# A store of 13 rows is sent as seven blocks of partitions

## The chip, the cores and the metric

The kernel runs on one core of a Trainium2 chip. The metric is device time in microseconds of one execution. A core has compute engines (TensorE or PE, VectorE or DVE, ScalarE or ACT, GpSimd or POOL), a queue engine SyncE or SP that issues transfers here, and 16 DMA engines that move data between HBM and SBUF. SBUF has 128 partitions.

## The reference

A channel attention: the mean over all pixels of each channel is scaled by one weight, put through a sigmoid, and multiplied into the input.

```python
g = jnp.einsum("bhwc->bc", x) / (H * W)
gp = jnp.pad(g, ((0, 0), (pad, pad)))
s = jnp.zeros_like(g)
for i in range(k):
    s = s + gp[:, i:i + C] * w1d[i]
s = _sigmoid(s)
return x * s[:, None, None, :]
```

`x` is bfloat16 of 1 x 384 x 384 x 384, 113.25 MB; `k` is 1. The output has the same shape. No output can be written before all of `x` has been read once, and `x` does not fit into SBUF as it is.

## The kernel before, in words

The 147,456 pixels are dealt to the 128 partitions, 1152 to each; the kernel calls one pixel of every partition a row, so a row is 128 x 384 bfloat16 values, 98,304 bytes, 768 bytes in a partition. One large SBUF tile, `arena`, has 275 rows. The rows are split into two chunks: `STREAMED` rows (785) are read twice, `KEPT` rows (367) are read once and stay on the chip, most of them with four rows folded into three (`fold`, and `unfold` in pass two), 71 of them raw.

Pass one loads everything and sums it on TensorE (`sum_rows`, L253), while DVE and ACT fold the kept rows. Then one sigmoid gives the scale `s_bf` (L443). Pass two (from L451) multiplies rows in place with `scale` (DVE, three pieces on POOL) and writes them out with `store`; rows that become free are filled by `load` with streamed rows, which are scaled and stored in turn.

The order of pass two comes from the planner loop at L688. It steps a model clock `now` in units of `DT`, with its own costs (`ROW`, `PER_STORE`, `TT`, `TS`), and decides what DVE does next and when SP issues which load or store. Every transfer of pass two is issued by SP, in the order in which the planner made it, through one queue. `landed` holds the rows ready to be scaled: first `Y`, `U`, `T` and `V` (4 or 8 rows each), then the first two slots of 13 rows, at `A` and `A + 13`. `send` puts a store in `waiting`, and L714 takes it from there when the model's DVE is done.

`Flow.add` (L34) works out what each step waits for from the arena rows that it reads and writes: a load waits for every earlier store that reads the rows that it overwrites. Each transfer has one of 24 semaphore lanes, and waits for the transfer 24 before it (L50). Waits of a transfer stand in SP's queue ahead of it (L111), so what is behind waits too. A transfer's semaphore rises by 16 and is complete when all of its DMA engines have landed their share.

The store of the change is the first of 13 rows in pass two: chunk `KEPT`, arena rows `A` to `A + 13`, `lo == raw(A)`. In the profile it is the ninth store of pass two, issued by SP at 278.31 us. Behind it SP issues a load of 8 rows (278.69 us), the 5 rows that POOL scaled (279.54 us), the next 13-row store (280.98 us), a load of 8 rows (281.90 us), and the load of 13 rows that overwrites the slot of the changed store (284.53 us), which waits for that store's landing.

Of the kernel before, what the change touches and what calls it, by code (L numbers as in the profile page):

```python
# [127 lines left out]
def kernel(  # L128
# [11 lines left out]
    nc = tc.nc  # L140
    P = nc.NUM_PARTITIONS
# [18 lines left out]
    A = V + PAIR  # L160
# [27 lines left out]
    arena = pool.tile([P, ROWS, C], bf16, name="arena")  # L188
# [11 lines left out]
    of = out.rearrange("b h w c -> (b h w) c")  # L200

    def view(t, r0, n):
        return t[r0 * P : (r0 + n) * P, :].rearrange("(p r) c -> p r c", r=n)

    def rows(lo, n):
        return [("a", r) for r in range(lo, lo + n)]

    fl = Flow(nc, tc)
# [6 lines left out]
    STREAMED, KEPT = (0, N_STREAM), (N_STREAM, N_KEPT)  # L215
# [8 lines left out]
    def raw(a):  # L224

        return c_raw + (a - U if a < G0 else PAIR + a - V)
# [65 lines left out]
    def fold(k):  # L292
# [46 lines left out]
        reads=["ones", "w_bf"], writes=["bank0"],  # L339
# [4 lines left out]
        reads=["bank0"], writes=["w_sc"],  # L344
# [39 lines left out]
    def copy_bank(i, src, dst, reads, writes):  # L384
        fl.add(
            "ACT", lambda: nc.scalar.copy(dst.bitcast(u32), src.bitcast(u32)), reads=reads, writes=writes  # L386
        )

    for i, bk in enumerate(banks):
        lo, hi = i * BANK, min((i + 1) * BANK, PS * C)  # L390
# [46 lines left out]
    for a, n in S2 + [(U, 8)] + S3 + S1 + [(V, 8), (Y, 8), (T, 5), (T + 5, 3)]:  # L437
# [6 lines left out]
        reads=["bank0", "w_sc"], writes=["s_bf"],  # L444
# [6 lines left out]
    def scale(a, n, eng="DVE", s=s_bf, after=()):  # L451
        v = arena[:, a : a + n, :]
        vec = nc.vector if eng == "DVE" else nc.gpsimd
        fl.add(
            eng,
            lambda: vec.tensor_tensor(  # L456
                out=v, in0=v, in1=s[:, None, :].to_broadcast([P, n, C]), op=Op.mult
            ),
            reads=rows(a, n) + ["s_bf" if s is s_bf else "bank0"], writes=rows(a, n), after=after,
        )  # L460

    def store(chunk, a, lo, hi):
        r0, n = chunk
        return fl.add(
            "SP",
            lambda: nc.sync.dma_start(out=view(of, r0, n)[:, lo:hi, :], in_=arena[:, a : a + hi - lo, :]),
            reads=rows(a, hi - lo), dma=True,
        )

    def unfold(k, first):  # L470

# [36 lines left out]
    def TT(n):  # L508
        return 0.15 + 0.2 * n
# [70 lines left out]
    def runs():  # L580
        got, i = [], 0
        while i < ROWS:
            if idle[i]:
                j = i
                while j < ROWS and idle[j]:
                    j += 1
                got.append((j - i, i))
                i = j
            else:
                i += 1  # L590
        return got

    def send(chunk, a, lo, hi, then, known=None):

        waiting.append((dve_at, hi - lo, then, chunk, a, lo, [] if known is None else known))

    def backlog():
        return sum(e[1] for e in moves) + ROW * sum(e[1] for e in waiting)
# [10 lines left out]
    def stored(a, n):  # L609

        def f():
            for i in range(a, a + n):
                for left in needed:
                    left.discard(("a", i))
                if not Y <= i < Y + 8 and not U <= i < U + 8 and not V <= i < V + 8:
                    idle[i] = True
        return f
# [30 lines left out]
    def start_group():  # L648

        if not line:  # L650
            return False
        g = line[0]
        column = home[g]
        if needed[column] or not free[column] or g == BANKED and (bank_at is None or now < bank_at[1]):
            return False
        line.popleft()
        free[column] = False
        a, q = GROUPS[g]
        if g == BANKED:
            a = bank_at[0]  # L660

        below = 0
        if column < 2 and g != COLUMNS[column][0]:
            below = GROUPS[COLUMNS[column][COLUMNS[column].index(g) - 1]][1]

        def part():
            release(a + below, sent - below)

        def done():
            nonlocal out_rows  # L670
            out_rows += 1
            free[column] = True
            release(a + max(below, sent), 4 * q - max(below, sent))

        for k in of_group(g):
            fields, three, fourth = unfold(k, a)
            turns.extend((fields + (None,), three + (None,), fourth + (None,)))
        sent = 0
        if len(line) >= total - N_SPLIT and q == PAIR:

            f, t, _ = turns[-5]
            sent = 3 * PIECE
            turns[-5] = (f, t, lambda: send(KEPT, a, c_group[g], c_group[g] + sent, part, written))
        f, t, _ = turns[-1]
        turns[-1] = (f, t, lambda: send(KEPT, a + sent, c_group[g] + sent, c_group[g] + 4 * q, done, written))
        return True

    while True:  # L688

        if dve_at <= now:  # L690
            ahead = backlog()
            can = bool(turns)
            if not can and not alongside and (ahead >= PENDING or not landed):
                can = start_group()
            if landed and (ahead < PENDING or not can):
                chunk, a, lo, n, end = landed.popleft()
                scale(a, n, s=s_ps if alongside and now else s_bf)
                dve_at = now + TT(n)
                since = (a, lo) if since is None else since
                if end or ahead < MERGE:  # L700
                    b, first = since
                    send(chunk, b, first, lo + n, stored(b, lo + n - first))
                    since = None
            elif can:
                f, t, then = turns.popleft()
                f()
                dve_at = now + t
                if then:
                    then()
        if alongside and alongside[0][0] <= now:  # L710
            _, chunk, a, lo, n = alongside.popleft()
            store(chunk, a, lo, lo + n)
            moves.append([now + LAT, n * ROW + PER_STORE, stored(a, n)])
        while waiting and waiting[0][0] <= now:  # L714
            _, n, then, chunk, a, lo, known = waiting.popleft()
            known.append(store(chunk, a, lo, lo + n))
            moves.append([now + LAT, n * ROW + PER_STORE, then])
        if not asked and not line and not turns:
            verdict()
            asked = True  # L720
        if out_rows == total and not checked:
            checked = True
            fl.add("POOL", again, reads=["odd_i", "s_bf"], writes=rows(Y, N_OVER), after=written)
        while over and over[0][0] <= now:
            over.popleft()[1]()

        got = runs()
        if bank_at is None and len(line) <= total - BANKS_AT and got and max(got)[0] >= PS * 4 // 3:
            a = max(got)[1]
            for i in range(a, a + PS * 4 // 3):  # L730
                idle[i] = False
            back = arena[:, a : a + PS, :].rearrange("p r c -> p (r c)")
            for i, bk in enumerate(banks):
                lo, hi = i * BANK, min((i + 1) * BANK, PS * C)
                copy_bank(i, bk[:, 0 : hi - lo], back[:, lo:hi], [("bank", i)], rows(a, PS))
            bank_at = (a, now + 5.0)
            got = runs()

        if got and todo < N_STREAM:
            n, a = max(got)  # L740
            n = min(n, CAP, N_STREAM - todo)
            ahead = backlog()
            if n >= BIG or n == N_STREAM - todo or (ahead < LOW and n >= 8) or ahead < LAST:
                load(STREAMED, a, todo, todo + n)
                for i in range(a, a + n):
                    idle[i] = False
                parts = [(STREAMED, a + e, todo + e, f - e, f == n) for e, f in split(n, PART)]
                todo += n
                moves.append([now + LAT, n * ROW + PER_LOAD, lambda parts=parts: landed.extend(parts)])

        if moves and moves[0][0] <= now:
            moves[0][1] -= DT
            if moves[0][1] <= 0:
                over.append((now + SEEN, moves.popleft()[2]))
        else:
            stall += DT
        if not (alongside or moves or waiting or over or landed or line or turns) and todo == N_STREAM:
            break
        now += DT
# [34 lines left out]
```

## Time and profile before

| What | Value |
|---|---|
| Time, median of 3 runs | 720.96 us (720.65, 720.96, 723.42) |
| Span of the profiled execution, first to last instruction | 719.4 us |
| Its own time outside the span | not recorded; the median is 1.6 us over the span |
| HBM read, written | 190.41 MB, 113.25 MB |
| Mean rate over the span | 422 GB/s |
| Busy: DVE, PE, ACT | 69%, 30%, 16% |
| Last landing of pass one; sigmoid | 267.1 us; 268.1 us |
| First store of pass two issued | 269.73 us |
| Changed store: issued, landed | 278.31 us, 284.5 us |
| Last store: issued, landed | 681.40 us, 717.6 us |

How to read it: times are from the start of the span. A stretch of the span has the busy time of each engine, the share of time for which the 16 DMA engines were busy on the mean, and the rate at which they moved bytes. A transfer has its issue in SP's queue, and a landing, which is that of its last DMA engine. The trace also holds a record for each landing of each transfer (one per DMA engine, without the engine's number) and for each packet (here one partition's part of a transfer).

### The profile page before, as it was taken

The page shows a single profiled execution, that of the slowest core. Times are in us where ns is not written, and L with a number is a line of the kernel's source. Part 1 is how long each engine was busy: PE and PEld are TensorE (multiplying, and loading weights), DVE is VectorE, ACT ScalarE, POOL GpSimd, SP SyncE. Part 2 cuts the span into 40 slices and gives each one's busy share as a digit, 9 for nine tenths or more (in the row PEclk, how much of TensorE's full clock was granted, in tenths as well). Part 3 has the DMA queues.
Part 4 walks back from the last instruction along what each step waited for, and adds up shares of the span by engine and source line. Part 5 has one row for each costly group of instructions (what it writes and reads, how often), then busy time and mean ns, then how long its engine had stood idle before and what let it go on. Part 6 is the DMA issues. An engine that isn't in the chain of part 4 may idle for free.

```text
span 719.4 us, 2061 instructions
## 1 busy us (share of the span) xinstructions
PE 213.0 (30%) x1202; PEld 0.3 (0%) x3; DVE 493.9 (69%) x471; ACT 115.7 (16%) x93; POOL 10.6 (1%) x7
## 2 busy tenths in 40 slices
PE   4677788897987770000000000000000000000000
PEld 0000000000000000000000000000000000000000
DVE  4600004788999719988999998999998985095500
ACT  3600003566677610002000000000000000000000
POOL 0000000000000005000000000000000000000000
PEclk9899999999999995555555555555555555555555
DMA  9999999999999979999999999999999999999997
GB/s 379 435 433 435 426 428 435 438 434 425 426 426 429 427 326 376 421 391 423 430 430 437 430 428 441 428 433 435 430 436 433 429 437 428 441 432 427 440 439 314
DMA packets 20174, 303.79 MB, mean 422 GB/s; under 512 B 2243, under 2 KB 2243, under 8 KB 6083
## 3 DMA queue, kind: packets, MB, share of 16 engines
q1 hardware_dynamic: 20160, 303.67, 99.0%
q8 instruction: 4, 0.07, 0.0%
q14 instruction: 8, 0.06, 0.0%
q10 hardware_dynamic: 2, 0.00, 0.0%
HBM read 190.41 MB, written 113.25 MB: 422 GB/s over the span
## 4 chain that ended last, share of the span: by engine, by line
DMA 63%; DVE 23%; PE 6%; ACT 2%; another core or an unknown queue 1%; SPq 1%; issue 0%; DVEq 0%
DMA arena<-in_x_dram 42%; DMA out_dram<-arena 20%; DVE arena L456 16%; PE bank L242 6%; DVE arena L276 4%; DVE arena L282 3%; ACT arena L313 2%; SPq L236 1%; ACT s_bf L443 0%; SPq L789 0%; DVEq L112 0%; SPq L106 0%
## 5 line engine op out<-in xcount | busy, mean ns | idle before, releaser
L456 DVE TENSOR_TENSOR arena<-arena,s_bf 128x4608 bf16<-128x4608 bf16 (+8 forms) x97 | 228.7, 2390 | 68.2 <-DMA arena<-in_x_dram 52.2
L276 DVE TENSOR_SCALAR arena<-arena 128x1536 uint16<-128x1536 uint16 (+2 forms) x247 | 145.3, 633 | 111.6 <-DMA arena<-in_x_dram 101.8
L242 PE MATMUL bank<-arena,ones 128*128 128x384 bf16 x1151 | 204.6, 339 | 46.3 <-DMA arena<-in_x_dram 46.3
L313 ACT ACTIVATE arena<-arena 128x3072 uint16<-128x3072 uint16 (+1 forms) x38 | 102.4, 2696 | 142.1 <-DVE arena L276 142.1
L282 DVE TENSOR_TENSOR arena<-arena 128x1536 uint16<-128x1536 uint16 (+2 forms) x114 | 121.0, 1061 | 5.2 <-PE bank L242 2.8
L529 PE MATMUL bank<-odd,ones 128*128 128x1 bf16 x1 | 0.2, 187 | 322.6 <-DVE odd L524 322.6
L456 POOL TENSOR_TENSOR arena<-arena,s_bf 128x1536 bf16<-128x1536 bf16 (+1 forms) x3 | 10.4, 3481 | 268.7 <-ACT bank L447 268.7
L386 ACT COPY arena<-bank 128x512 uint32<-128x512 uint32 (+1 forms) x7 | 4.0, 570 | 58.2 <-DMA out_dram<-arena 58.1
L456 DVE TENSOR_TENSOR arena<-arena,bank 128x1536 bf16<-128x1536 bf16 (+2 forms) x7 | 11.3, 1689 | 0.0
L242 PE MATMUL bank<-zeros,ones 128*128 128x384 bf16 x48 | 8.3, 326 | 0.0
L313 ACT ACTIVATION_READ_ACCUMULATOR arena<-arena 128x1 f32 x38 | 7.1, 186 | 0.0
L386 ACT COPY bank<-arena 128x512 uint32<-128x512 uint32 (+1 forms) x7 | 3.6, 567 | 0.0
L443 ACT ACTIVATE s_bf<-bank,w_sc 128x384 bf16<-128x384 f32 x1 | 0.6, 580 | 14.5 <-PE bank L242 14.5
L256 PE MATMUL bank<-arena,ones 128*128 128x384 bf16 x1 | 0.5, 480 | 6.8 <-DMA arena<-in_x_dram 6.8
L762 ACT ACT_TABLE_LOAD x1 | 1.3, 1283 | 0.7 <-PEq L778 0.7
L343 DVE TENSOR_SCALAR w_sc<-bank 128x1 f32<-128x1 f32 x1 | 0.2, 157 | 1.2 <-PE bank L338 1.2
L333 DVE MEMSET ones<- 128x128 bf16 x1 | 0.2, 165 | 1.0 <-SPq L106 1.0
L338 PE MATMUL bank<-w_bf,ones 1*128 1x1 bf16 x1 | 0.2, 179 | 2.2 <-DMA w_bf<-in_w1d_dram 2.2
L529 PEld LDWEIGHTS bank<-odd,ones 128*128 128x128 bf16 x1 | 0.1, 105 | 581.5 <-DVE odd L524 581.5
L533 DVE CAST odd_i<-bank 128x1 int32<-128x1 f32 x1 | 0.2, 157 | 0.3 <-PE bank L529 0.3
L447 ACT COPY bank<-s_bf 128x192 uint32<-128x192 uint32 x1 | 0.3, 322 | 0.0
L519 DVE TENSOR_REDUCE worst<-seen 128x1 f32<-128x38 f32 x1 | 0.2, 186 | 0.0
(8 smaller groups left out, 0.9 us busy)
## 6 DMA issues: line engine op xcount, KB each, us to landing
arena<-in_x_dram SPq DMA_DIRECT2D x15, 4608.0 KB, 34.8
arena<-in_x_dram SPq DMA_DIRECT2D x21, 1248.0 KB, 13.5
out_dram<-arena SPq DMA_DIRECT2D x7, 3072.0 KB, 33.1
arena<-in_x_dram SPq DMA_DIRECT2D x6, 3072.0 KB, 27.5
out_dram<-arena SPq DMA_DIRECT2D x4, 4608.0 KB, 39.3
arena<-in_x_dram SPq DMA_DIRECT2D x6, 2304.0 KB, 18.5
arena<-in_x_dram SPq DMA_DIRECT2D x3, 4512.0 KB, 27.1
out_dram<-arena SPq DMA_DIRECT2D x10, 1248.0 KB, 11.9
```

Of the source, the lines that this page charges most:

```text
L236: lambda: nc.sync.dma_start(out=arena[:, a : a + hi - lo, :], in_=view(xf, r0, n)[:, lo:hi, :]),
L242: return pe.add_instruction(mybir.InstMatmult(name=nc.get_next_instruction_name(), ins=[pe.lower_ap(rhs), pe.lower_ap(ones[:])], outs=[pe. ...
L256: return nc.tensor.matmul(acc, lhsT=ones[:], rhs=arena[:, i, :], start=first, stop=last)
L276: lambda: nc.vector.tensor_scalar(out=dst, in0=src, scalar1=s0, scalar2=s1, op0=op0, op1=op1),
L282: "DVE", lambda: nc.vector.tensor_tensor(out=dst, in0=a, in1=b, op=op), reads=reads, writes=writes
L313: lambda: nc.scalar.activation(out=y, in_=y, func=ACTF.Copy, accum_out=seen[:, 2 * k + i : 2 * k + i + 1]),
L386: "ACT", lambda: nc.scalar.copy(dst.bitcast(u32), src.bitcast(u32)), reads=reads, writes=writes
L443: lambda: nc.scalar.activation(out=s_bf[:], in_=acc, func=ACTF.Sigmoid, scale=w_sc[:, 0:1]),
L447: "ACT", lambda: nc.scalar.copy(s_ps.bitcast(u32), s_bf[:].bitcast(u32)), reads=["s_bf"], writes=["bank0"]
L456: lambda: vec.tensor_tensor(out=v, in0=v, in1=s[:, None, :].to_broadcast([P, n, C]), op=Op.mult),
L529: lambda: nc.tensor.matmul(votes, lhsT=ones[:], rhs=odd[:], start=True, stop=True),
L762: nc.scalar.preload_act_table(ACTF.Sigmoid)
```

## The change

The first 13-row store of pass two is issued as seven transfers, one for each block of partitions: 80, 14, 12, 9, 7, 4 and 2. Together they write the same bytes. By the description of the change the first block is shared by all 16 DMA engines, 5 partitions for each, and each smaller block gives one partition to each of as many engines, so that the engines have 11 down to 5 partitions each in place of 8. All other stores stay as they are (`WHOLE`). The planner's model of the store is unchanged, and so is the order of all other steps. The load that overwrites the slot waits for all seven.

```diff
-    def store(chunk, a, lo, hi):
+    WHOLE, STAIRS = (P,), (80, 14, 12, 9, 7, 4, 2)
+    assert sum(STAIRS) == P
+
+    def store(chunk, a, lo, hi, blocks=WHOLE):
         r0, n = chunk
-        return fl.add(
-            "SP",
-            lambda: nc.sync.dma_start(out=view(of, r0, n)[:, lo:hi, :], in_=arena[:, a : a + hi - lo, :]),
-            reads=rows(a, hi - lo), dma=True,
-        )
+        sent, p0 = [], 0
+        for b in blocks:
+            p = slice(p0, p0 + b)
+            sent.append(
+                fl.add(
+                    "SP",
+                    lambda p=p: nc.sync.dma_start(
+                        out=view(of, r0, n)[p, lo:hi, :], in_=arena[p, a : a + hi - lo, :]
+                    ),
+                    reads=rows(a, hi - lo), dma=True,
+                )
+            )
+            p0 += b
+        return sent
...
             _, n, then, chunk, a, lo, known = waiting.popleft()
-            known.append(store(chunk, a, lo, lo + n))
+            blocks = STAIRS if chunk is KEPT and lo == raw(A) else WHOLE
+            known.extend(store(chunk, a, lo, lo + n, blocks))
```

## The prediction

> **What bounds the kernel now.** I read the stages first, by busy time per stretch of pass two (columns: from:to, length, then PE, PEld, DVE, ACT and POOL busy with their counts, granted clock, DMA busy share, GB/s):
>
> ```profile
> 278.20:281.80 3.60, 0.00 (x0) 0.00 (x0) 3.60 (x4) 0.00 (x0) 1.32 (x1) 0.50 1.00 416
> 281.80:284.00 2.20, 0.00 (x0) 0.00 (x0) 2.17 (x5) 0.00 (x0) 0.00 (x0) 0.50 0.99 249
> 284.00:320.00 36.00, 0.00 (x0) 0.00 (x0) 33.28 (x31) 0.00 (x0) 0.00 (x0) 0.50 1.00 403
> 320.00:434.00 114.00, 0.00 (x0) 0.00 (x0) 109.62 (x99) 3.99 (x7) 0.00 (x0) 0.50 1.01 431
> 434.00:700.00 266.00, 0.19 (x1) 0.10 (x1) 197.29 (x138) 0.00 (x0) 0.00 (x0) 0.50 1.01 434
> 700.00:719.40 19.40, 0.00 (x0) 0.00 (x0) 0.00 (x0) 0.00 (x0) 0.00 (x0) 0.50 0.75 322
> ```
>
> From 320 us to the end the 16 DMA engines are always busy, at 431 to 434 GB/s, as in pass one (425 to 438 in its slices after the first). That is 27.1 GB/s for one engine. DVE has 69 us to spare after 434 us. So nothing after 320 us can get faster or slower except that all engines arrive there earlier or later: the end is the state at 320 us plus a fixed amount of bytes. Only 278 to 320 us is below the ceiling. The changed store is issued at the start of it, in the SP queue:
>
> ```profile
> 278.31 0.33 SPq L466 DMA_DIRECT2D out_dram<-arena  x1
> 278.69 0.54 SPq L236 DMA_DIRECT2D arena<-in_x_dram  x1
> 279.54 2.26 SPq L466 DMA_DIRECT2D out_dram<-arena  x2
> 281.90 2.96 SPq L236 DMA_DIRECT2D arena<-in_x_dram  x2
> ```
>
> The second load of the last line (issued 284.53) overwrites the slot that the changed store reads, and waits for it. The issues by line, asked for the window of that store and of the load behind it, give the time from issue to the last engine's landing:
>
> ```profile
> out_dram<-arena SPq DMA_DIRECT2D x1, 1248.0 KB, 6.2
> arena<-in_x_dram SPq DMA_DIRECT2D x1, 768.0 KB, 9.2
> ```
>
> So the store lands at 278.31 + 6.2 = 284.5 and the load at 278.69 + 9.2 = 287.9. Last, the chain of waits through the rest of the stage:
>
> ```profile
> 300.52 9.96 DMA out_dram<-arena
> 310.48 0.02 issue
> 310.50 0.33 SPq L236
> 310.82 0.04 issue
> 310.87 11.61 DMA out_dram<-arena
> ```
>
> A load waits in SP until 310.48 for the last engine of an older store. Engines that were done early have nothing to do meanwhile; the latest engine never waits. So **the latest engine's own path sets the end.** The trace's landing records (16 for each transfer, one per engine) show how far it lags: the 16 landings lie within 0.49 us for the changed store, 1.85 for the load behind it, 2.95 for the load issued at 292.16, 4.06 for that of 307.62, 2.99 for that of 310.50 (last one at 319.48), and 3.03 for the last store of all. There the last is 1.85 us behind the mean. After 319.48 the lag is simply carried to the end.
>
> How much the latest engine has lost: from the landing of the store ahead (280.49) to 319.48 are 38.99 us. In them land 13+8+5+13+8+13+12+13+8+8+13+5+8+8+13 = 148 rows of 98,304 bytes (128 partitions of 768), 14.55 MB, at 434 GB/s 33.5 us. **5.5 us are lost on the latest engine, the most that any change to this stage can win.**
>
> **The change part by part.**
>
> The ramp. One partition of the store is 13 x 768 = 9984 bytes, at 27.1 GB/s 0.37 us. Before, each engine has 8 of them, 2.95 us; after, 11 down to 5, 4.06 down to 1.84. So an engine is shifted by +1.1 to -1.1 us, none on the mean. Which engine is the latest is not shown by any record of before (landings carry no engine number), so the ramp's cost at the end lies between -1.1 and +1.1, and I take 0, the middle.
>
> SP's issues. Six more. In this stage an issue takes 0.33 us at the least (278.31) and, in the records of this queue, up to 0.94 (281.90): 2.0 to 5.6 us more, and everything in SP behind is moved: the load of 278.69, the 5-row store that POOL scaled, the next 13-row store and two loads, each on the same queue. No engine's instruction waits for these before 311.81 (DVE's first idle time on a load), and DVE goes on scaling. What hides the delay is the work already queued: the packet records start the store at 280.0, so the lightest engines (5 partitions) are busy until 281.8 and the heaviest until 284.1. At 0.33 each the load goes out at 280.7, and 1.7 us later (as 278.31 to 280.0) it is at the engines, 282.4: the lightest idle 0.6 us, the heaviest not at all. At 0.94 each it is there at 286.0: the lightest idle 4.2 us, and the heaviest are held back too, since their last block arrives at 285.6 instead of being reached at 283.7, 1.9 us. So 0 to +1.9 on the latest engine; I take +0.3, near the low end, because most issues of 278 to 311 us took 0.33 to 0.49.
>
> Waits. The load into the slot waits for seven landings in place of one; SP's extra wait instructions are hundredths of a us (0.02 in the chain). The last block lands with the heaviest engine, 1.1 us later, 285.6 instead of 284.5. Behind this load SP has nothing until 289.32, when a store waits for DVE, and at 284.5 the engines still have 34 rows queued (7.7 us): covered, 0. If the store slipped by over 7 us, that cover would be gone.
>
> Lanes. A transfer waits for the one 24 before it on its semaphore lane; with six more the window is 18 old transfers. The oldest that this reaches are stores landed by 280 us for issues after 310 us: 0.
>
> DVE, ACT, PE, POOL: the same instructions in the same order, 0.
>
> **Sum.** 0 (ramp) + 0.3 (issues) + 0 (waits, lanes) = +0.3 us on the profiled execution's span of 719.4: 719.7. The median of the runs, 720.96, is 1.6 over that span, so 721.3, about 0.05% more. The profiled execution's time outside its span isn't recorded; 1.6 stands for it.
>
> [...]
>
> **The rivals.**
>
> *Faster: the ramp spares the engines their falling out of step.* The stage loses time while the engines go in step (landings within 0.5 us at 284.5), and none once they are 3 us apart. If this is cause and effect, a ramp of 2.2 us given at the start spares it. Then the latest engine is 1.1 us behind the mean in place of 1.85 (-0.75), and the wait of 310.48, after which the next load's first landing comes 1.15 us later than its bytes explain (landing records), mostly goes with other losses of the mean: -1.5 together. -2.3: 718.7. Against it: eight engines land within 0.45 us of each other after 319 us and lose nothing. It decides if the load behind the store has no engine over 1.1 us behind the mean. All 5.5 us less the ramp's 1.1 would give 716.6, the far end.
>
> *Slower: the blocks' engines get in each other's way,* being on neighbouring partitions as they have not been before. Price by the row: at 249 in place of 416 GB/s, 11 partitions take 4.06 x 1.67 = 6.8 us, 2.7 more; with half of the 0.3 to 1.1 from issues and ramp about +3: 724. [...] It decides if the seven blocks take over 6 us from first packet to last landing, and nothing later gives it back. [...]
>
> *The change doesn't do what it says:* blocks of 14, 12, 9, 7, 4 and 2 go to one engine each time. Then one engine has 5 + 48 partitions, 45 more than now, 16.6 us: 738. The change's description speaks against it; no transfer of before shows how such a count is shared out.
>
> **How the numbers follow.** No change that a measurement of this kernel can tell is about 0.5%, 3.6 us: 717.4 to 724.6. Forecast (721.3, its own range 719.8 to 722.8): 0.44. Faster rival: 0.27, of which 0.09 beyond 717.4. Slower rival: 0.26, of which 0.13 beyond 724.6. Not as said: 0.03. Chances: faster 0.09, within 0.74, slower 0.17. The range leaves out about 0.08 below and 0.12 above: 717.6 to 725.0.
>
> **What would show it.** Right: the stretch from 320 us at 431 to 434 GB/s as now; seven issues of 0.33 to 0.49; the slot's load issued 1 to 2 us later, near 286; last landing within 1.5 us of now. Wrong: that load issued after 288 (blocks in each other's way), or issues near 0.9 us; the state at 320 us more than 2 us earlier, with a landing spread near 2 us in the loads before it (faster rival); a rate after 320 us other than now, which would break the ground of the whole sum.

## The result, and the profile after

| | Before | Changed |
|---|---|---|
| Median of 8 runs each, us | 721.65 (720.65 to 723.42) | 724.81 (723.31 to 726.38) |
| Ratio, 95% interval | 1 | 1.0041 (1.0027 to 1.0055) |
| Span of the profiled execution, us | 719.4 | 723.4 |

The changed kernel is 0.41% slower, about 3.0 us, and the interval lies clear of 1. The loss is inside the 0.5% that the prediction counts as no change, and 724.81 is inside its range of 717.6 to 725.0, but close to the upper end, and the forecast of 721.3 was too low.

The stretches of the changed kernel, as they were shown of before (columns: from:to, length, PE, PEld, DVE, ACT and POOL busy, granted clock, DMA busy share, GB/s):

```profile
278.20:281.80 3.60, 0.00 (x0) 0.00 (x0) 3.60 (x4) 0.00 (x0) 1.73 (x1) 0.50 1.03 371
281.80:284.00 2.20, 0.00 (x0) 0.00 (x0) 2.17 (x5) 0.00 (x0) 0.00 (x0) 0.50 0.79 186
284.00:320.00 36.00, 0.00 (x0) 0.00 (x0) 30.16 (x29) 0.00 (x0) 0.00 (x0) 0.50 0.96 381
320.00:434.00 114.00, 0.00 (x0) 0.00 (x0) 109.53 (x94) 4.00 (x7) 0.00 (x0) 0.50 1.01 429
434.00:700.00 266.00, 0.18 (x1) 0.10 (x1) 201.15 (x145) 0.00 (x0) 0.00 (x0) 0.50 1.01 433
```

From 320 us on nothing has changed to speak of (429 and 433 against 431 and 434 GB/s). The loss lies between 278 and 320 us: 371, 186 and 381 GB/s against 416, 249 and 403. In 281.8 to 284.0 the DMA engines are now idle for a fifth of the time, and for longer behind it, as 284 to 290 us shows, first before and then changed:

```profile
284.00:290.00 6.00, 0.00 (x0) 0.00 (x0) 6.00 (x5) 0.00 (x0) 0.00 (x0) 0.50 1.02 408
```

```profile
284.00:290.00 6.00, 0.00 (x0) 0.00 (x0) 5.72 (x5) 0.00 (x0) 0.00 (x0) 0.50 0.69 175
```

SP's queue at that place, and below it the issues by line for the windows of the block of 80 and of the load behind the store (time from issue to landing at the end of the line):

```profile
278.74 6.50 SPq L475 DMA_DIRECT2D out_dram<-arena  x7
285.29 1.06 SPq L236 DMA_DIRECT2D arena<-in_x_dram  x1
286.40 0.90 SPq L475 DMA_DIRECT2D out_dram<-arena  x2
287.41 1.99 SPq L236 DMA_DIRECT2D arena<-in_x_dram  x2
```

```profile
out_dram<-arena SPq DMA_DIRECT2D x1, 780.0 KB, 6.2
```

```profile
arena<-in_x_dram SPq DMA_DIRECT2D x1, 768.0 KB, 7.6
```

The changed execution is 0.42 us late already at its first store (270.15 against 269.73), which is not the change's doing. The seven issues take 6.5 us; single ones take up to 2.4 us (that of 9 partitions) and 1.8 us (that of 7). The load behind the store goes out at 285.29 instead of 278.69 and lands at 292.9 instead of 287.9. And the block of 80 alone, 62% of the bytes, lands 6.2 us after its issue, as late as the whole store did before. By the landing records its first engine is done at 282.86 and its last at 284.93, 2.07 us apart, where the whole store's engines were 0.49 us apart. The last of the small blocks lands at 288.6.

The chain of waits further on has kept its form:

```profile
289.06 12.85 DMA arena<-in_x_dram
301.91 0.02 issue
301.93 2.77 DVE arena L456
304.70 0.02 issue
304.72 9.48 DMA out_dram<-arena
314.20 0.02 issue
314.22 0.33 SPq L236
```

The load that overwrites the slot goes out at 289.06 (before 284.53). The load that waited until 310.48 for an older store's last engine now waits until 314.20, 3.3 us later when the 0.42 are taken off. That is most of the loss, and it is carried to the end. There the 16 landings of the last store lie within 3.93 us, the last one 3.08 behind their mean (before 3.03 and 1.85), and that last one comes at 721.9 instead of 717.6, 4.3 us later.

The packet records tell where the 4.3 us went. From 278.2 to 320 us the engines have no packet under way for 2.0 us more than before, on the mean of the 16. Packets take 0.5 us more for each engine than the same sizes take undisturbed (a packet of 9984 bytes takes 0.375 us in the kernel before after 355 us). At the end the last engine is 1.2 us further behind the mean, and 0.4 us is the late start, which makes 4.1. So the idle time is the largest part here; the 0.5 us of stretched packets is not clear of chance, because the same sum differs by up to 0.9 us between profiles of kernels that are alike in this stage (before, and the four kernels below that change only a later store).

### The profile page after: what moved, and what is told of

Read it like the earlier page. It is cut to its first block, busy times and chain, and to the rows that moved or that the text cites. A ratio compares the mean times of both kernels' runs of the same rounds, so it can differ in the third digit from the quotient of the medians.

```text
span 723.4 us, 2071 instructions
## 1 busy us (share of the span) xinstructions
PE 214.2 (30%) x1202; PEld 0.3 (0%) x3; DVE 494.0 (68%) x471; ACT 115.7 (16%) x93; POOL 10.6 (1%) x7
## 4 chain that ended last, share of the span: by engine, by line
DMA 62%; DVE 22%; PE 5%; ACT 3%; another core or an unknown queue 1%; SPq 1%; issue 0%; DVEq 0%
DMA arena<-in_x_dram 42%; DMA out_dram<-arena 20%; DVE arena L456 15%; DVE arena L276 5%; PE bank L242 5%; DVE arena L282 3%; ACT arena L313 3%; SPq L236 1%; ACT s_bf L443 0%; SPq L112 0%; DVEq L112 0%; SPq L475 0%; SPq L804 0%; SPq L106 0%
```

## The experiments

Two theories stood at the start. **Issue theory:** SP needs 6.5 us for seven issues, the transfers behind them come late, and the engines run dry. **Sharing theory:** a block of neighbouring partitions moves slowly, because its engines are in each other's way. The third, **ramp theory**, was that the engines with 11 partitions simply end later. Diffs are against the changed kernel; ratios are against the kernel before, on the same chips.

### Two blocks instead of seven

```diff
-    WHOLE, STAIRS = (P,), (80, 14, 12, 9, 7, 4, 2)
+    WHOLE, STAIRS = (P,), (80, 48)
```

> The store goes as two blocks of 80 and 48 partitions, 5 and 3 for each engine: no ramp, one issue more than before instead of six. Issue theory (the changed kernel is 3 us slower because SP spends 6.5 us on the seven issues, 278.74 to 285.29, and the load behind them comes when the engines have run dry): SP spends about 0.7 to 1.1 us, the load behind goes out by 279.9, and the time is 0 to 0.8 us over before. Sharing theory (a block of neighbouring partitions moves slowly, since the engines are in each other's way; the landings of the block of 80 in the changed kernel are 2.08 us apart, those of the whole store before 0.49): the block of 80 is as slow as there, the 48 as well, the store's last landing comes 8 us or more after its issue instead of 6.2, and the time is 1.5 to 3 us over before. Ramp theory (engines with 11 partitions end later): nothing, 0.

Measured: 1.0019 (1.0009 to 1.0029), 1.4 us. The queue and the window of the two blocks:

```profile
278.52 0.89 SPq L475 DMA_DIRECT2D out_dram<-arena  x2
279.45 1.66 SPq L236 DMA_DIRECT2D arena<-in_x_dram  x1
281.16 4.37 SPq L475 DMA_DIRECT2D out_dram<-arena  x2
285.62 1.56 SPq L236 DMA_DIRECT2D arena<-in_x_dram  x1
```

```profile
out_dram<-arena SPq DMA_DIRECT2D x1, 780.0 KB, 6.0
out_dram<-arena SPq DMA_DIRECT2D x1, 468.0 KB, 9.5
```

The load behind goes out by 279.5, as the issue theory said, and the kernel is slower all the same. The store's last landing is 278.9 + 9.5 = 288.4, 9.9 us after its first issue against 6.2 before. The time is just under the sharing theory's lower bound. By the packet records the engines were idle no longer than before (0.2 us less from 278.2 to 320 us), and their packets took 1.5 us more for each engine. What nobody expected: the *whole* transfers behind the two blocks now take 1.6 to 2.4 us each to issue. So a slow issue can be a sign of engines that are held up, and not the cause.

### Seven transfers of all partitions

```diff
+        if blocks is STAIRS:
+            for e, f in split(hi - lo, 2):
+                sent += store(chunk, a + e, lo + e, lo + f)
+            return sent
         for b in blocks:
```

> The store goes as seven transfers of all 128 partitions, of 1 or 2 rows each: six issues more as in the changed kernel, no ramp, and each engine on its usual partitions. Issue theory: if an issue is slow here because there are seven of them, SP is held for 4 to 6.5 us and the time is 2 to 3.5 us over before; if it is slow because of the shape of the blocks, the seven take 0.33 to 0.6 each, 2.3 to 4 us in all, and the time is 0.5 to 1.5 over before. Sharing theory: no sharing, so only SP's 2.3 us at least, 0 to 0.7 over before. Ramp theory: 0.

Measured: 0.9992 (0.9983 to 1.0002).

```profile
278.50 3.38 SPq L479 DMA_DIRECT2D out_dram<-arena  x7
281.94 0.45 SPq L236 DMA_DIRECT2D arena<-in_x_dram  x1
282.43 0.96 SPq L479 DMA_DIRECT2D out_dram<-arena  x2
283.50 0.75 SPq L236 DMA_DIRECT2D arena<-in_x_dram  x1
```

Seven issues take 3.4 us, the load behind is issued 3.2 us later than before, and it costs nothing. So the number of issues is not the cause, and a delay of 3 us at this place is covered by what is queued. The issue theory is left with the slow issues alone.

### The small blocks from another queue

```diff
-                    "SP",
-                    lambda p=p: nc.sync.dma_start(
+                    "ACT" if blocks is STAIRS and p0 else "SP",
+                    lambda p=p, q=nc.scalar if blocks is STAIRS and p0 else nc.sync: q.dma_start(
```

> The block of 80 stays in SP's queue, the six small ones are issued by ACT, which has nothing else to do until 327 us. The blocks, the ramp and the sharing are those of the changed kernel; only SP is free for the load behind at 278.7 to 279.1. Issue theory: the time goes back to within 1 us of before, and the stretch 281.8 to 284.0 has its engines busy again (0.95 or more instead of 0.79). Sharing theory: the time stays 2 to 3.5 us over before. Ramp theory: 1 us over before, with landings 2 us or more apart from the load behind the store on.

Measured: 1.0055 (1.0032 to 1.0079), no better than the changed kernel.

```profile
278.23 0.35 SPq L475 DMA_DIRECT2D out_dram<-arena  x1
278.23 6.88 ACTq L475 DMA_DIRECT2D out_dram<-arena  x6
278.62 0.50 SPq L236 DMA_DIRECT2D arena<-in_x_dram  x1
279.45 4.38 SPq L475 DMA_DIRECT2D out_dram<-arena  x2
283.93 1.61 SPq L236 DMA_DIRECT2D arena<-in_x_dram  x1
```

The load behind goes out at 278.62, at its old place, and the issue theory, as an account of the whole loss, falls with it: the first load's queue wait was taken away and the loss stayed. While the blocks are under way, both queues issue slowly, ACT 6.9 us for six, SP 4.4 for two whole stores. The stretch 281.8 to 284.0 moves 172 GB/s with its engines 0.93 busy: slow rather than idle. The packet records say the same of 278.2 to 320 us: no more idle time than before, and 2.6 us more in stretched packets for each engine. In the changed kernel it was 2.0 us idle and 0.5 us stretched. So the blocks cost either way: with SP held up behind them the engines run dry, and with SP free their packets take longer.

### The small blocks behind other transfers

```diff
+        if blocks is STAIRS:
+            later.append([len(fl.queued["SP"]) + 1 + BEHIND, lambda: store(chunk, a, lo, hi, STAIRS[1:], STAIRS[0])])
+            blocks = STAIRS[:1]
...
+        if later and len(fl.queued["SP"]) >= later[0][0]:
+            later.popleft()[1]()
```

> The block of 80 is issued in its place, the six small ones in SP's queue behind the next four transfers (load 8, store 5, store 13, load 8), just ahead of the load that overwrites the slot. The same blocks with the same shares and the same number of issues; only what stands behind them in SP's queue is less. Issue theory: 34 rows (7.7 us) are queued at the engines while SP issues the six, so the time is within 1 us of before. Sharing theory: the blocks are as slow as now, 2 to 3.5 us over before. Ramp theory: 1 us over before.

Measured: 1.0085 (1.0067 to 1.0104), worse than any theory said. The reason is a new wait that the edit itself makes:

```profile
284.35 5.14 SPq L481 DMA_DIRECT2D out_dram<-arena  x6
296.42 0.37 SPq L236 DMA_DIRECT2D arena<-in_x_dram  x1
```

```profile
284.00:300.00 16.00, 0.00 (x0) 0.00 (x0) 13.63 (x14) 0.00 (x0) 0.00 (x0) 0.50 0.74 277
```

The small blocks stand behind 34 rows on the engines, so the last of them lands at 296.4, and the load that overwrites the slot, with everything behind it in SP's queue, waits until 296.42. The engines are idle for a quarter of 284 to 300. This run doesn't tell the two theories apart.

### Lone stores

A kernel with nothing but these stores, each after the landing of the one before:

```python
SETS = [  # first partition, step, how many
    (0, 1, 128), (0, 1, 80), (0, 1, 64), (0, 2, 64), (80, 1, 48), (0, 1, 32), (0, 4, 32), (0, 1, 16), (0, 8, 16),
    (0, 1, 8), (0, 4, 8), (0, 1, 4), (0, 4, 4), (0, 32, 4), (80, 1, 14), (115, 1, 7), (126, 1, 2), (0, 1, 1),
]
```

> A kernel of its own that leaves the whole computation out: SBUF is filled with ones, and stores of 13 rows (9984 bytes a partition) go out one at a time, each after the one before has landed, from 18 sets of partitions, twice. It measures the sharing by itself. [...] If the partitions' place does not matter, and only each engine's own count does: the 80 take 1.5 more than one partition, the 64 take 1.1, the 32 0.37, and every set of 16 or fewer takes 0 more, near or apart.

Measured: "whole" is the time from one issue to the next, "packets" that from the start of the store's first packet to the end of its last, by the packet records (the second pass through the list agrees within 0.06 us).

| Partitions | Whole, us | Packets, us |
|---|---|---|
| 128 | 4.47 | 3.21 |
| 80 neighbours | 4.91 | 3.72 |
| 64 neighbours | 4.80 | 3.22 |
| 64, every 2nd | 3.21 | 1.68 |
| 48 neighbours | 4.30 | 3.11 |
| 32 neighbours | 2.85 | 1.66 |
| 32, every 4th | 2.42 | 0.90 |
| 16 neighbours | 2.83 | 1.65 |
| 16, every 8th | 2.41 | 0.85 |
| 14 neighbours | 2.80 | 1.62 |
| 8 neighbours | 2.70 | 1.58 |
| 8, every 4th | 2.15 | 0.44 |
| 7 neighbours | 2.68 | 1.56 |
| 4 neighbours | 2.64 | 1.56 |
| 4, every 4th | 2.06 | 0.44 |
| 4, every 32nd | 2.29 | 0.78 |
| 2 neighbours | 1.85 | 0.78 |
| 1 | 1.43 | 0.375 |

The issues by line for the windows of the 128, the 80 and the 64 neighbours, and the queue's issues of 16 apart, 8 neighbours, 8 apart, 4 neighbours, 4 apart and 4 at every 32nd:

```profile
out_dram<-arena SPq DMA_DIRECT2D x1, 1248.0 KB, 4.5
```

```profile
out_dram<-arena SPq DMA_DIRECT2D x1, 780.0 KB, 4.9
```

```profile
out_dram<-arena SPq DMA_DIRECT2D x1, 624.0 KB, 4.8
```

```profile
36.08 0.53 SPq L160 DMA_DIRECT2D out_dram<-arena  x1
38.49 0.33 SPq L160 DMA_DIRECT2D out_dram<-arena  x1
41.19 0.73 SPq L160 DMA_DIRECT2D out_dram<-arena  x1
43.34 0.25 SPq L160 DMA_DIRECT2D out_dram<-arena  x1
45.98 0.64 SPq L160 DMA_DIRECT2D out_dram<-arena  x1
48.04 0.52 SPq L160 DMA_DIRECT2D out_dram<-arena  x1
```

These are blocks of partitions alone, with no other transfer under way. The block of 80 takes *longer* than the whole store (4.9 against 4.5 us), and the 64 neighbours take longer than twice their bytes, while every second partition takes 3.2. Eight neighbours take 2.70 and eight that lie 4 apart 2.15, with the same bytes. Four that lie 32 apart are in between (2.29, against 2.64 for four neighbours and 2.06 for four that lie 4 apart). The packet records put these in the same order: 1.56 us for four neighbours, 0.78 for four that lie 32 apart, 0.44 for four that lie 4 apart. Of neighbours, 7 to 32 take hardly more than four, 1.56 to 1.66. If only the number of partitions counted for each engine, every set of 16 or fewer would take as long as one partition, 0.375; eight that lie 4 apart come near to that, and eight neighbours, with 1.58, do not. Single packets show the same: 0.375 us for one partition alone and for four that lie 4 apart, 0.73 to 0.74 for two neighbours, 1.16 to 1.34 for four. So the time of a store's packets goes with which partitions it takes, and not with their number alone. By what mechanism is not shown, nor why the packets of the block of 80 take 0.5 us longer than those of all 128 (3.72 against 3.21).

The whole times differ by less than the packets' times, because some stores start later: the first packet comes 0.7 to 0.9 us after the start of the issue for the 128, the single one and the neighbours other than the 64, and 1.15 to 1.4 us after it for the 64 neighbours and the sets with gaps. So four neighbours cost 0.58 us more than four that lie 4 apart in whole time, and 1.12 in packets. The late start is also why four partitions apart take 0.6 us more than one.

One rival is left: the places in HBM that a store writes move with its partitions, and no run moves the one without the other. The packets' times follow which partitions are stored; whether that is due to SBUF, to HBM or to both is not shown.

### Blocks of 16, neighbours and apart

```diff
-            p = slice(p0, p0 + b)
+            p = slice(16 * j, 16 * j + 16) if blocks is STAIRS else slice(0, P)
```

and the same with `slice(j, 128, 8)`; `STAIRS` is `(16,) * 8`, `j` the number of the block.

> The store goes as eight blocks of 16 neighbouring partitions, one for each engine in every block: 8 partitions for each engine as before, no ramp, eight issues. [...] Issue theory (dead already by the seven transfers of all partitions, which cost nothing): eight issues of 0.45, 0 to 1 over before.

> The same with the 16 partitions of a block 8 apart: the same number of issues, the same shapes and shares, only other partitions in each block. [...] If the place does not matter: the same as with the neighbours.

Measured: 1.0025 (1.0012 to 1.0038) for the neighbours, 1.0014 (1.0003 to 1.0025) for those 8 apart. Both lose, the neighbours more, but the difference is only 0.8 us, and the intervals overlap. SP needs 5.7 us for the eight issues of the neighbours and 5.3 us for those apart, so that part of the loss may be SP's. There is no ramp in either: the ramp is not needed for a loss.

### The stairs where nothing waits for them

```diff
-            blocks = STAIRS if chunk is KEPT and lo == raw(A) else WHOLE
+            thirteens[0] += n == 13 and chunk is STREAMED
+            blocks = STAIRS if n == 13 and chunk is STREAMED and thirteens[0] == LATE else WHOLE
```

`LATE` is 6: the store that the kernel before issues at 354.46.

> The first 13-row store stays whole; the seven blocks of the changed kernel go on a later store, that which before issues at 354.46, with 6 to 9 us of work queued at every engine and no load of the same slot soon behind. What SP spends and who waits is hidden here; what the engines lose is not, since they are never idle after 320 us. Waiting theory (the loss is the engines run dry because what is behind the blocks is issued late): within 1 us of before. Sharing theory: the engines themselves lose 1.5 to 4 us, and the time is that much over before. Ramp theory: the landings of all later transfers are spread anew by up to 2.2 us, and the time is -1 to +1.

Measured: 1.0040 (1.0015 to 1.0065), about the loss of the early place. The times are spread far more widely than those of any other kernel here, from 721.9 to 730.1 us around a median of 724.3, and the profiled execution (726.9) is one of the longer ones. This kernel's queue, then the stretches that follow, of before (first pair) and of this kernel (second):

```profile
354.96 2.81 SPq L476 DMA_DIRECT2D out_dram<-arena  x7
357.87 0.37 SPq L236 DMA_DIRECT2D arena<-in_x_dram  x1
```

```profile
360.00:375.00 15.00, 0.00 (x0) 0.00 (x0) 14.28 (x13) 0.00 (x0) 0.00 (x0) 0.50 1.02 436
375.00:434.00 59.00, 0.00 (x0) 0.00 (x0) 57.87 (x55) 0.00 (x0) 0.00 (x0) 0.50 1.01 432
```

```profile
360.00:375.00 15.00, 0.00 (x0) 0.00 (x0) 11.94 (x12) 0.00 (x0) 0.00 (x0) 0.50 1.01 408
375.00:434.00 59.00, 0.00 (x0) 0.00 (x0) 56.44 (x49) 0.00 (x0) 0.00 (x0) 0.50 1.01 425
```

The issues are quick here (2.8 us for seven), the engines are busy throughout (1.01), and yet they move 408 GB/s instead of 436. Neither waiting nor running dry is left; the engines themselves are slower. From 345 to 434 us no packet of before is stretched; here packets take 1.55 us more for each engine than their sizes take undisturbed. The landings, 3.1 us apart before the blocks, are 7.6 apart in the load behind them and 5.5 at the end.

### What of the blocks costs: neighbours, apart, or only their number

At the same late place: the two kinds of blocks of 16 as above, and the store as seven transfers of all partitions (the edit of the second experiment).

> Eight blocks of 16 neighbouring partitions on the later store (that of 354.46 in the kernel before), where the blocks of the changed kernel, put there, cost 0.4%. Every engine has one partition in each block, 8 in all: no ramp, and nothing in SP's queue that the engines could run dry for. Sharing theory: in the lone stores 16 neighbours took 2.83 us and 16 partitions 8 apart 2.41, 0.42 us more a block, 3.4 us for eight one after the other; the engines lose 1 to 3.4 us each, the rate of 360 to 375 falls below 420 GB/s, and the time is 1 to 4 us over before. If the ramp or the uneven blocks were what cost in the changed kernel: within 1 us of before.

> The same with the 16 partitions of each block 8 apart. [...] If it is the number or the shape of the blocks and not their place: the same as with the neighbours.

> The later store (354.46 in the kernel before) as seven transfers of all 128 partitions, of 1 or 2 rows each: as many transfers as the changed kernel's blocks, at the place where those cost 0.4% and eight blocks of 16 cost 0.31% (neighbours) and 0.22% (8 apart), but every engine stays with the partitions that it has in a whole store. Sharing theory: nothing is lost, within 0.7 us of before, and 360 to 375 runs at 425 GB/s or more. If it is the number of transfers or their short packets: 1.5 to 3 us over before, as with the blocks of 16.

Measured: neighbours 1.0031 (1.0018 to 1.0045), 8 apart 1.0022 (1.0012 to 1.0033), all partitions 1.0000 (0.9991 to 1.0009). The stretch behind the store, in this order:

```profile
360.00:375.00 15.00, 0.00 (x0) 0.00 (x0) 12.39 (x12) 0.00 (x0) 0.00 (x0) 0.50 1.01 397
```

```profile
360.00:375.00 15.00, 0.00 (x0) 0.00 (x0) 12.91 (x12) 0.00 (x0) 0.00 (x0) 0.50 1.03 404
```

```profile
360.00:375.00 15.00, 0.00 (x0) 0.00 (x0) 13.91 (x13) 0.00 (x0) 0.00 (x0) 0.50 1.03 425
```

Seven transfers of the same bytes cost nothing as long as each has all 128 partitions. (Their 425 GB/s against 436 before is the packets of 1536 bytes, which take 0.065 us where that share of a packet of 9984 bytes would take 0.058: 0.4 us for each engine by an estimate from these two, which is inside the interval.) Eight blocks of partitions, even with equal shares, cost 1.6 to 2.2 us. So it is which partitions a transfer takes that costs. The packet records bear this out: from 345 to 380 us each engine loses 1.5 us to stretched packets with neighbours, 1.2 us with those 8 apart, and 0.00 us with all partitions, as before.

The difference between the two kinds of blocks is only 0.65 us, within the intervals. Blocks of partitions 8 apart still lose most of it. It is not their own packets that are slow: packets of the store's size, 9984 bytes, lose 0.8 us for each engine with neighbours, but 0.1 us with those 8 apart. The rest, 0.6 and 1.1 us, is lost in the packets of the two loads issued behind the blocks, which are whole transfers again, and most of it after the last block has landed (367.7 and 366.8 us). The engines are further out of step there (landings 4 to 5 us apart instead of 3), but why that slows the loads' packets is not shown.

### A try for a faster kernel

The first pair of lines is against the second experiment, the last line against the changed kernel:

```diff
-            for e, f in split(hi - lo, 2):
+            for e, f in split(hi - lo, 4):
...
+            blocks = STAIRS if n >= 12 and now < 40 else WHOLE
```

> Not a test of the cause but a try for a faster kernel. The seven transfers of all partitions cost nothing and raised the stretch 281.8 to 284.0 from 249 to 349 GB/s, at -0.08% of the time with an interval that just holds 0. Here the four stores of 12 or 13 rows that are issued between 278 and 301 us go in pieces of 3 or 4 rows of all partitions. If the smaller packets are what helps there: 0.5 to 2 us under before. If it was chance, or the extra issues (each 0.45 us) hold the loads up: 0 to 1 over.

Measured: 1.0035 (1.0023 to 1.0048), 2.5 us over and worse than either expectation. 284 to 320 us fell to 377 GB/s, and the issues between 278 and 286 us took 0.5 to 1.0 us each after the first. Why four split stores cost this much, when one cost nothing, is not shown. The 0.08% of the single split store is not told from chance. No version here beats the kernel before.

## Why the prediction was right, and where it was wrong

- **The ground of the sum held.** After 320 us the rate is as before, and the end moved by what the stage from 278 to 320 us lost. (The 5.5 us of the prediction were the most that a change could win there; they set no bound to a loss.)
- **The step that failed is the sum's "0 (ramp) + 0.3 (issues)".** Measured in those terms: behind the late issues the engines were idle for 2.0 us more on the mean, just over the upper end of the prediction's 0 to +1.9; the lag of the last engine, put at 0, grew by 1.2 us; and stretched packets, for which the sum had no term, took 0.5 us, not clear of chance. Seven whole transfers brought none of this, so what the sum lacked is the price of blocks of partitions. The signs that the prediction had set for being wrong were met: the seven issues took 0.93 us each on the mean, and the slot's load went out at 289.06, after the 288 that was named. The last landing came 4.3 us later, not within 1.5.
- **The time fell inside the range through the slower rival, and its price was partly luck.** The rival, blocks in each other's way, was the right one: its price was about +3 us and 724, and 3.0 us and 724.8 were measured. Its deciding point was met: the blocks take 8.2 us from their first packet (280.4) to the last landing (288.6), over the 6 that were named. But it priced slow packets at 2.7 us and half of the issues and ramp beside it, where most of the changed kernel's loss was idle time and lag. With SP free, slow packets did take the 2.6 us.
- **The weighing chose the wrong side.** The rival was held at 0.26 while no row of before showed a partial store. The lone stores price one: for the block of 80, 5 partitions an engine, the prediction's price for a partition gave 1.84 us; its packets take 3.7 us alone, and from issue to landing it takes 4.9 us, the whole store 4.45. That half of the rival's chance lay beyond 724.6 was the author's estimate, which no run shows.
- **Issues: size wrong, cause wrong.** Six more issues were bounded at 2.0 to 5.6 us; they took 6.2. But 3.4 us for seven whole transfers cost nothing, and taking the small blocks out of SP's queue gained nothing. The long issues came with the slow blocks, on both queues. (The bound of 1.9 us counts all seven issues at 0.94, the 286.0 beside it only six; counted alike it is 1.3.)
- **Waits: the 0 held.** The slot's load went out 4.5 us late, but the transfers queued ahead of it land until 298.8. The idle time lies earlier, between the blocks and the load of 8 rows behind them, which came 6.6 us late: that is the issues' term.
- **Ramp: not seen as such.** In the load behind the store, 15 of 16 engines land within 0.97 us of each other, and the last one 1.87 us behind the mean, so the faster rival's deciding point (none over 1.1) was not met. That the idle time evened out a ramp of 2.2 is likely, but not shown. Where the stairs stood in a deep queue, the engines did spread, to 7.6 us, and the time rose by 0.40%: spreading the engines gained nothing there.
- **"The change doesn't do what it says":** it does. Behind the blocks the landing records show 14, 12, 9, 7, 4 and 2 landings, one per engine, and one record more right after each issue.

## What to carry to other kernels

Where the DMA engines are the bound and one transfer has to be split, split it by what each partition holds (rows), not by partitions: seven transfers of all 128 partitions cost nothing at either place here, eight of 16 partitions 0.14 to 0.31%. That is no leave to split freely, since four stores split by rows cost 0.35%. A long issue in a DMA queue can be a symptom; see whether moving it to another queue helps before it is called the cause (here ACT took 6.9 us for six, and the loss stayed). And when the row that would price an operation is missing, measure it alone, and read its packets: 18 lone stores told more than the four experiments before them.

## What the runs showed that was not expected

- An issue of an ordinary whole transfer takes 1.6 to 2.4 us while blocks of partitions are under way (two blocks, 279.45 to 287.2), where the same four took 0.5 to 0.9 us before. A second queue does not escape it (ACT, 6.9 us for six). In a deep queue the same seven blocks were issued in 2.8 us. What holds the issue up is not shown.
- Half the partitions, as neighbours, take longer to store than all of them (4.8 against 4.45 us). Their packets take as long (3.22 against 3.21 us), and the first one starts 0.3 us later.
- The stretch 281.8 to 284.0 rose from 249 to 349 GB/s when its 13-row store went in pieces of 1 or 2 rows. The 292 with four stores cut says nothing: the profiles of the four kernels that change only the later store show 223 to 290 GB/s there. In all of these five the packets of the whole 13-row store take 0.49 us each on the mean, instead of 0.375 later on. Why they are slow just there stays open.
